# Two attentions on one core: first tokens in halves, late clearing of padding, a finer last tile

## The chip, the cores and the metric

The kernel runs on one NeuronCore of a Trainium2 chip. The core has a matrix engine (TensorE, "PE" in the profile), three engines for elementwise work (VectorE "DVE", ScalarE "ACT", GpSimd "POOL"), and a queue engine (SyncE, "SP") that issues most of the transfers. TensorE writes to PSUM[...]. The metric is the device time of one execution in microseconds, and the median of several runs is given.

## The reference

The kernel computes two attention layers, A and B, over 2048 tokens with width 640 and 32 heads of 20 columns, and puts their outputs side by side (2048 x 1280, bf16).

```python
# A: four segments of 512 tokens, causal inside a segment, with a memory M, z of the segments before
for s in range(N):
    p = softmax(qs @ ks.T * scale + causal_mask)
    a_mem = (phi(qs) @ M) / (phi(qs) @ z + 1e-06)
    o = g * a_mem + (1.0 - g) * (p @ vs)          # g = sigmoid(beta), one for each head
    M, z = M + phi(ks).T @ vs, z + sum(phi(ks))
A = concat(o) @ wo
# B: a sliding window of 256 tokens
p = softmax(where((0 <= i - j) & (i - j < 256), q @ k.T * scale, -1e9))
B = (p @ v) @ wo
```

`phi(t)` is `t + 1` where `t > 0`, else `exp(t)`.

## The kernel before

Tokens are cut into eight chunks of 512, in the order A0, B0, A1, B1, A2, B2, A3, B3. The 32 heads form eight groups of four heads (`G = 8`), and a "half" of a chunk is four groups. Nine phases each hold one or two of these halves: phase 0 is A0's first half, phase 1 is A0's second half with B0's first half, and so on to phase 8, which is B3's second half alone. `SHIFT` says how far the second half-chunk of a phase is put behind the first when their batches are interleaved.

The chain for a group of heads is this.
- **Projections.** `x` times the weights gives queries and keys with the head columns on the partitions, and values with tokens on the partitions. For most groups, queries and keys go through a store to a scratch tensor in DRAM and a spread of four loads, which puts each head on 32 partitions (`qk_job`, `bounce`). The first four groups of A0 use weights that are already padded to 32 columns a head (`wkd`, `wqd`), so they are cast directly into `kA` and `qA` (`proj_direct`).
- **Scores.** `score_batch` (L706) multiplies up to 512 columns for each of four heads into two PSUM tiles `sc`. ScalarE exponentiates each of the two (L717) into a tile `pt`. There are three `sc` tiles and six `pt` buffers (`NSC`, `NPT`). GpSimd then clears what the masks exclude (`mask`, L763 and L767).
- **Values.** `av` (L781) multiplies `pt` by the values, which carry a column of ones, so that the sum of the softmax comes out beside the result. `turn` (L804) transposes in blocks of 32 on VectorE. `norm` takes the reciprocal (L827) and multiplies (L822). `back` (L859) transposes back, and `final_job` (L895) or, for the last chunk, `last_job` (L930) does the output projection. `evac` (L235 on ScalarE, L237 on VectorE) copies PSUM to SBUF.
- **Last chunk.** Chunk B3 is handled by query tile of 128 tokens: `unit` makes three score batches of a half tile (a pair of groups with earlier keys, the diagonal blocks of all four groups, the second pair), and one "tile" entry follows them that takes the AV of the four groups into one bank, one turn of 512 columns and one norm.

All instructions are written out by a planner, which has a model of the time of each engine (`Flow`). `f.pe` is its TensorE clock. Jobs such as a projection are generators; at each step the planner takes the first job whose need is met at `f.pe`, a score batch when its keys and queries are marked done, or an AV when its masks are done. Constants named `T_W` are due times for work that waits for the first loads. `ORDER` holds one seed for each score batch. Where a seed is not zero, `pick` draws from a small random generator: it lets a job be passed over, holds a batch back, or shifts the comparison in `evac` that decides between ScalarE and VectorE. The order of each engine's queue is fixed once it is written.

The start is in `body`. SyncE loads the first chunk of `x` in three transfers (column tiles 0, 1 to 2, 3 to 4). ScalarE's queue issues the key and query weights of group 0, then `beta`. SyncE loads the padded weights of groups 1 to 3, then `wv_A`, `wk_A`, `wq_A`, the next `x` and the remaining weights. Twelve warm-up matmuls (L1157) run on a zeroed tile meanwhile. GpSimd and VectorE clear the padding of `kA`, `qA`, `qB`, `pqA`, `kB`, `MZb` and two edge tiles (L1164 to L1182), and GpSimd sets the ones in the value tiles (`v_tile`, L668 and L669). The constants made from `beta` (`consts_beta`, L304 to L320: one exponential on ScalarE and nine small VectorE instructions) and `epsv` (L289) are written out after the first planner step past `T_W[1]`.

Of the kernel before, what the change touches and what calls it, by code (L numbers as in the profile page):

```python
# [13 lines left out]
P = 128  # L14
# [14 lines left out]
    0, 768, 0, 845, 879, 493, 987, 701, 177, 0, 698, 208, 547, 919, 0, 0, 0, 989, 663, 0, 464,  # L29
    0, 0, 696, 205, 683, 935, 478, 935, 428, 909, 435, 0, 106, 0, 638, 428, 489, 780, 970, 630,  # L30
    137, 112, 487, 987, 852, 257, 438, 73, 0, 330, 618, 0, 747, 421, 0, 683, 0, 174, 542, 0,
    478, 0, 0, 0, 405, 92, 46, 310, 146, 369, 521, 643, 874, 863, 619, 683, 633, 393, 811, 875,
    892, 0, 124, 604, 814, 906, 281, 583, 0, 128, 0, 643, 307, 776, 926, 0, 727, 286, 730, 616,
    317, 955, 721, 602, 431, 787, 591, 819, 0, 635, 158, 0, 206, 0, 742, 0, 0, 232, 0, 0, 33,
    470, 435, 0, 281, 366, 583, 0, 816, 0, 0, 338, 402, 726, 607, 722, 643, 431, 417, 0, 671,
    258, 337, 208, 92, 687, 820, 129, 0, 876, 532, 783, 0, 474, 542, 646, 0, 284, 332, 0, 0,
    130, 0, 846, 102, 982, 640, 781, 0, 548, 590, 124, 838, 417, 75, 197, 0, 471, 465, 0, 331,
    690, 0, 0, 409, 0, 99, 655, 0,
)
STRETCH = 1  # L40
EW, EB = 3, 1
# [6 lines left out]
T_W = (5600.0, 7200.0, 12300.0, 12500.0, 14500.0, 16500.0)  # L48
SLACK = 500.0
SPREAD = 500.0  # L50
SHIFT = (0.0, 0.5, 0.0, 0.25, 0.0, 0.25, 0.5, 1.0, 0.0)
# [20 lines left out]
           ([(3, 6, 2, 0), (1, 2, 6, 128)], [("diag", 0, 128, 128)])]  # L72
WHOLE_B = [([(0, 0, 6, 128), (3, 6, 2, 0)], [("diag", 0, 128, 128), ("far", 384, 0, 128)]),
# [127 lines left out]
class _K:  # L201
# [149 lines left out]
    def proj_direct(self, n, w, xT, dst, g, what, ready):  # L351

        nc, f = self.nc, self.f
        yield ready
        yield "bank"
        ps, bi = self.bank()
        for kt in range(self.KT):
            nc.tensor.matmul(ps[:, :], lhsT=w[:, g, kt, :], rhs=xT[:, kt, :],
                             start=(kt == 0), stop=(kt == self.KT - 1))
            f.on_pe("full", mm_ns(512))  # L360
            if kt < self.KT - 1:
                yield 0.0
        t = self.evac(dst[:, g, :], ps[:, :], 512, 612.0)
        self.close(bi, t)
        f.open = False
        self.mark(t, n, what, g)
        self.used_x(n)
# [297 lines left out]
    def v_tile(self, name):  # L665
        v = self.big.tile([P, 2 * VH], BF16, name=name)
        for a in (0, VH):
            self.nc.gpsimd.memset(v[:, a:a + LT * VW].rearrange("p (t e) -> p t e", e=VS)[:, :, DH], 1.0)  # L668
            self.nc.gpsimd.memset(v[:, a + LT * VW:a + VH], 1.0)  # L669
        return v  # L670

    def score_batch(self, bt, kof, q):
# [43 lines left out]
        for i in range(2):  # L716
# [3 lines left out]
            self.sc_free.append(te)  # L720
        for m in masks:
            if halves:
# [30 lines left out]
    def mask(self, pt, te, kind, c0, d, w=64):  # L753

        nc, f = self.nc, self.f
        r = 8 if d else 4
# [3 lines left out]
        elif d:  # L760
            blk = pt[:].rearrange("p a (y c) -> p (a y) c", c=256)[:, :, c0:c0 + w]
# [36 lines left out]
    def turn(self, O, bi):  # L798
# [5 lines left out]
        self.nc.vector.transpose(out=tt[:], in_=O[:, :])  # L804
        self.close(bi, f.on_dve(640.0, f.pe + PE_OUT))
        return tt

    def norm(self, tt, dst, key, last):
# [3 lines left out]
        NB = L // HD  # L812
        tv = tt[:].rearrange("p (b c) -> p b c", c=HD)
        rr = self.wk.tile([P, NB], F32, name="rr", bufs=4)
        t = f.dve

        def part(out, ready=0.0):
            a, b = tv[:, :, 0:DH], rr[:].unsqueeze(2).to_broadcast([P, NB, DH])
# [5 lines left out]
            return f.on_dve(470.0, ready, True)  # L824

        def s1():
            nc.vector.reciprocal(out=rr[:], in_=tv[:, :, DH])  # L827
# [128 lines left out]
    def unit(self, n, half):  # L956
# [5 lines left out]
        if n == len(self.chunks) - 1:  # L962
            for i in range(LT):
                out = []
                if (n, half) in WHOLE:
                    for g in gs[::2]:
                        out.append([n, [(g1, (i - y, 2 * i, 2, 256 * x + 128 * (2 - y)))
                                        for x, g1 in enumerate((g, g + 1)) for y in (2, 1)],
                                    [("far", 0, 256, 128)], []])
                    out.insert(1, [n, [(g, (i, 2 * i, 2, 128 * x)) for x, g in enumerate(gs)],  # L970
                                   [("diag", 0, 256, 128), ("diag", 128, 256, 128)], []])
                    out[-1][3].append((i, gs[0]))
                    blocks.append(out)
                    continue
                for g in gs[::2]:
                    ents = []
                    for g1, c0 in ((g, 0), (g + 1, 256)):
                        ents += [(g1, (i - 2, 2 * i, 1, c0)), (g1, (i - 1, 2 * i, 2, c0 + 64)),
                                 (g1, (i, 2 * i + 1, 1, c0 + 192))]
                    out.append([n, ents, [("far", 0, 256), ("diag", 192, 256)], []])  # L980
                out.insert(1, [n, [(g, (None, i, i, 64 * x)) for x, g in enumerate(gs)],
                               [("half", 0)], []])
                out[-1][3].append((i, gs[0]))
# [482 lines left out]
```

## Time and profile before

| | |
|---|---|
| median of 8 runs | 360.54 us (360.04 to 362.11) |
| time of the profiled execution | 360.43 us |
| its span, first to last instruction | 358.4 us |
| ScalarE busy | 326.1 us (91%) |
| VectorE, GpSimd busy | 298.7 us, 222.2 us |
| first exponential of a score batch starts | 11.50 us |
| last exponential ends | 348.91 us |

A group's row in the page gives line, engine, operation, output and inputs with their shapes and the count; then busy time in us and mean ns of one; then the idle time of the engine just before and what ended it. A row of the timeline gives the start and the length in us, then the same names; a row with x5 covers five instructions that follow each other. A row of the waits gives the waiting engine and line, what ended the wait, the total in us, the number of waits and the longest.

### The profile page before, as it was taken

How to read it: one execution, taken by the hardware profiler on the slowest of the kernel's cores; microseconds unless marked ns; L12 is line 12 of the kernel's file. 1: busy time of each engine (PE TensorE's matmuls, PEld its weight loads, DVE VectorE, ACT ScalarE, POOL GpSimd, SP SyncE). 2: the span in 40 equal slices, each digit the busy share in tenths (PEclk: the TensorE clock that was granted, in tenths of full speed). 3: DMA queues.
4: the chain of work that ended last, by engine and by line, in shares of the span. 5: the costliest groups of instructions: out<-in, count | busy, mean ns of one | idle time of the engine just before them, and what ended most of it. 6: DMA issues, size and time to landing. Idle time of an engine off the chain costs nothing.

```text
span 358.4 us, 13242 instructions
## 1 busy us (share of the span) xinstructions
PE 332.5 (93%) x5515; PEld 165.9 (46%) x5515; DVE 298.7 (83%) x558; ACT 326.1 (91%) x367; POOL 222.2 (62%) x282
## 2 busy tenths in 40 slices
PE   8899999999999999989898999989999999989996
PEld 3334543544543544534433644444544544645564
DVE  6569687988998888998988987998996799899762
ACT  1797599999999999989989899999999999999991
POOL 8243146674756586492966839486269843987881
PEclk9999999999999999999999999999999999999999
DMA  7994656368374232672544203564334122112111
GB/s 243 393 380 136 194 153 167 111 194 197 103 230 115 85 98 77 211 196 84 171 148 123 64 16 98 157 163 134 102 100 142 52 80 83 52 47 90 65 50 38
DMA packets 45123, 47.90 MB, mean 134 GB/s; under 512 B 16312, under 2 KB 40696, under 8 KB 45064
## 3 DMA queue, kind: packets, MB, share of 16 engines
q1 hardware_dynamic: 44488, 46.65, 41.9%
q8 instruction: 43, 0.70, 0.9%
q10 hardware_dynamic: 576, 0.42, 0.4%
q14 instruction: 16, 0.13, 0.1%
HBM read 24.91 MB, written 19.14 MB: 123 GB/s over the span
## 4 chain that ended last, share of the span: by engine, by line
PE 48%; DVE 25%; ACT 16%; issue 6%; DMA 2%; POOL 1%; SPq 1%; ACTq 0%; DVEq 0%
ACT pt L717 15%; PE m L433 14%; PE sc L706 8%; PE m L895 8%; PE m L781 7%; PE m L619 5%; DVE tt L804 4%; DVE oD L859 3%; DVE st L237 3%; DVE o L822 2%; DVE vA L631 2%; DVE st L461 2%; DVE ot L237 2%; PE m L1057 2%; PE m L930 2%
## 5 line engine op out<-in xcount | busy, mean ns | idle before, releaser
L717 ACT ACTIVATE pt<-sc 128x1024 bf16<-128x1024 f32 (+1 forms) x344 | 307.8, 1023 | 12.1 <-PE sc L706 11.3
L767 POOL TENSOR_SCALAR_AFFINE_SELECT pt<-pt 128x512 bf16<-128x512 bf16 (+1 forms) x148 | 128.0, 868 | 124.7 <-ACT pt L717 123.7
L804 DVE STREAM_TRANSPOSE tt<-m 128x512 f32<-128x512 f32 x88 | 61.8, 709 | 20.7 <-PE m L781 19.0
L763 POOL TENSOR_SCALAR_AFFINE_SELECT pt<-pt 128x512 bf16<-128x512 bf16 (+1 forms) x80 | 72.0, 901 | 2.7 <-ACT pt L717 2.7
L237 DVE CAST st<-m 128x512 bf16<-128x512 f32 x74 | 50.2, 680 | 14.6 <-PE m L433 13.8
L706 PE MATMUL sc<-qB,kB 32*128 32x128 bf16 (+2 forms) x928 | 43.0, 248 | 3.2 <-ACT pt L717 2.5
L822 DVE TENSOR_TENSOR o<-tt,rr 128x320 bf16<-128x320 f32 x64 | 41.1, 643 | 0.5
L619 PEld LDWEIGHTS <-xT 128*128 128x128 bf16 x400 | 32.4, 97 | 17.5 <-issue 7.6
L706 PE MATMUL sc<-qA,kA 32*128 32x64 bf16 (+4 forms) x608 | 30.0, 261 | 2.1 <-DVE qA L237 1.5
L237 DVE CAST ot<-m 128x512 bf16<-128x512 f32 (+1 forms) x39 | 25.3, 650 | 6.9 <-PE m L895 4.2
L706 PEld LDWEIGHTS <-kB 32*128 32x128 bf16 x928 | 16.4, 92 | 31.4 <-issue 27.4
L895 PE MATMUL m<-wo_A,oD 128*128 128x512 bf16 (+1 forms) x160 | 26.0, 300 | 4.4 <-DVE vB L237 2.9
L895 PEld LDWEIGHTS <-oD 128*128 128x128 bf16 x280 | 19.6, 98 | 19.7 <-issue 8.2
L433 PE MATMUL m<-xT,wBq 128*128 128x512 bf16 x100 | 26.1, 380 | 2.1 <-DVE tt L804 0.7
L781 PE MATMUL m<-pt,vB 128*32 128x128 bf16 (+2 forms) x928 | 25.7, 250 | 1.9 <-DVE vA L631 0.6
L433 PE MATMUL m<-xT,wBk 128*128 128x512 bf16 x100 | 26.0, 380 | 1.6 <-DVE vA L631 0.9
L619 PE MATMUL m<-wBv,xT 128*128 128x320 bf16 (+2 forms) x200 | 26.6, 273 | 0.8 <-DVE tt L804 0.6
L619 PE MATMUL m<-wv_A,xT 128*128 128x320 bf16 (+2 forms) x200 | 26.2, 273 | 1.1 <-DVE vA L631 1.1
L781 PEld LDWEIGHTS <-vB 128*32 128x32 bf16 x928 | 17.6, 97 | 14.0 <-issue 4.5
L433 PE MATMUL m<-xT,wk_A 128*128 128x512 bf16 x90 | 23.3, 381 | 0.5 <-DVE tt L804 0.4
L859 DVE STREAM_TRANSPOSE oD<-o 128x512 bf16<-128x512 bf16 x35 | 23.4, 680 | 0.0
L781 PE MATMUL m<-pt,vA 128*32 128x448 bf16 (+5 forms) x608 | 22.2, 264 | 1.2 <-DVE st L237 1.0
(86 smaller groups left out, 363.5 us busy)
## 6 DMA issues: line engine op xcount, KB each, us to landing
out_dram<-ot SPq DMA_DIRECT2D x35, 128.0 KB
scr_kB<-st SPq DMA_DIRECT2D x20, 128.0 KB
scr_qB<-st SPq DMA_DIRECT2D x20, 128.0 KB
kB<-scr_kB SPq DMA_DIRECT2D x32, 80.0 KB
qB<-scr_qB SPq DMA_DIRECT2D x32, 80.0 KB
scr_kA<-st SPq DMA_DIRECT2D x18, 128.0 KB
scr_qA<-st SPq DMA_DIRECT2D x18, 128.0 KB
kA<-scr_kA SPq DMA_DIRECT2D x28, 80.0 KB
```

Source lines behind the costliest of these rows:

```text
L237: nc.vector.tensor_copy(out=out, in_=in_)
L433: nc.tensor.matmul(ps[:, :], lhsT=w_ap[:, kt, m * P:(m + 1) * P], rhs=xT[:, kt, :], start=(kt == 0), stop=(kt == self.KT - 1))
L619: nc.tensor.matmul(ps[:, c0:c0 + w], lhsT=xT[:, kt, tt * P:(tt + 1) * P], rhs=w_ap[:, kt, a:a + w], start=(kt == 0), stop=(kt == self.KT - 1))
L706: nc.tensor.matmul(ps[j // 2][:, j % 2, c0:c0 + 64 * nb], lhsT=k[rows, g, P * kc:P * kc + P], rhs=q[rows, g, 64 * b0:64 * (b0 + nb)], star ...
L717: nc.scalar.activation(out=pt[:, 2 * i:2 * i + 2, 0:hi], in_=ps[i][:, :, 0:hi], func=ACT.Exp, scale=self.scale)
L763: nc.gpsimd.affine_select(out=blk, in_=blk, pattern=[[0, r], [-1, w]], compare_op=ALU.is_ge, fill=self.zero, base=-1, channel_multiplier=1)
L767: nc.gpsimd.affine_select(out=blk, in_=blk, pattern=[[0, r], [1, w]], compare_op=ALU.is_ge, fill=self.zero, base=128 - w, channel_multipli ...
L781: nc.tensor.matmul(O[HD * j:HD * j + HD, c:c + 64 * nb], lhsT=self.vcols(v, h // 16 if vk[0] == "v" else 0, vt, h, HD), rhs=rhs[j], start= ...
L804: self.nc.vector.transpose(out=tt[:], in_=O[:, :])
L822: nc.vector.tensor_tensor(out=out, in0=a, in1=b, op=ALU.mult)
L859: self.nc.vector.transpose(out=self.oD[n][:, x:y, b0:b0 + nb, :].rearrange("p c b t -> p b c t"), in_=o[:, b0:b0 + nb, :].rearrange("p b ( ...
L895: nc.tensor.matmul(ps[:, P * y:P * y + w], lhsT=self.oD[n][:, m, LT * qt:LT * qt + LT, :] .rearrange("p b t -> p (b t)"), rhs=wo[:, m, a:a ...
```

## The change

The first chunk of `x` is loaded as 256 columns first (two transfers) and the other 256 columns after (one). Keys and queries of group 0 are projected in two column halves, with due times `T_W[0]` and `T_X`. A new list `FIRST` divides group 0 into three score batches, the first of which needs only the first half; group 1 gets a batch of its own for the block that it shared with group 0. Four warm-up matmuls are left out. `wv_A` is loaded after `wk_A` and `wq_A`. The jobs of A0's two halves are put into one list in the order `INIT`.

The clearing of `qB`, `pqA`, `MZb`, `kB[1]` and the edge tiles, and the ones of the `vB` tiles, go to a list `late` that is sorted by due time: each entry is written out when `f.pe` passes it. `kB[1]` and the edge tiles move from VectorE to GpSimd. `consts_beta` and `consts_eps` are in the same list.

For the last chunk, the diagonal batch comes first in each tile, also in its first half. In the last tile of the last half, the AV, turn, norm and back are done for two groups at a time, and the last mask is applied to each pair of heads after its exponential. `ORDER`, four entries of `SHIFT` and the other constants of the planner have new values.

```diff
-T_W = (5600.0, 7200.0, 12300.0, 12500.0, 14500.0, 16500.0)
+T_W = (3700.0, 6200.0, 15000.0, 10900.0, 12900.0, 16500.0)
+T_X = 5300.0
-SHIFT = (0.0, 0.5, 0.0, 0.25, 0.0, 0.25, 0.5, 1.0, 0.0)
+SHIFT = (0.0, 0.5, 0.25, 0.25, 1.0, 0.0, 0.75, 1.0, 0.0)
+INIT = ("p1", "v0", "p2", "p3", "k1", "q1", "v1")
+FIRST = [([(0, 0, 4, 0), (1, 2, 2, 256)], [("diag", 0, 256, 128)]),
+         ([(0, 4, 4, 0), (1, 4, 4, 256)], []),
+         ([(3, 6, 2, 0), (2, 4, 4, 128)], [("diag", 0, 128, 128)])]
...
-    def proj_direct(self, n, w, xT, dst, g, what, ready):
+    def proj_direct(self, n, w, xT, dst, g, what, ready, a=0, b=L):
...
-            nc.tensor.matmul(ps[:, :], lhsT=w[:, g, kt, :], rhs=xT[:, kt, :],
+            nc.tensor.matmul(ps[:, 0:b - a], lhsT=w[:, g, kt, :], rhs=xT[:, kt, a:b],
                              start=(kt == 0), stop=(kt == self.KT - 1))
...
-        t = self.evac(dst[:, g, :], ps[:, :], 512, 612.0)
+        t = self.evac(dst[:, g, a:b], ps[:, 0:b - a], b - a, 80.0 + 1.04 * (b - a))
...
+            if masks and len(masks[-1]) == 5:
+                tm = self.mask(pt, te, *masks[-1][:4], hs=(2 * i, 2 * i + 2))
...
-    def turn(self, O, bi):
+    def turn(self, O, bi, w=L):
...
+                out.append([n, [(g, (i, 2 * i, 2, 128 * x)) for x, g in enumerate(gs)],
+                            [("diag", 0, 256, 128), ("diag", 128, 256, 128)], []])
                 for g in gs[::2]:
...
+                    end = i == LT - 1 and half == 1 and g == gs[2]
+                    out.append([n, [(g1, (i - y, 2 * i, 2, 256 * x + 128 * (2 - y)))
+                                    for x, g1 in enumerate((g, g + 1)) for y in (2, 1)],
+                                [("far", 0, 256, 128) + ((1,) if end else ())], []])
+                    if end:
+                        out[-2][3].append((i, gs[0], 2))
+                        out[-1][3].append((i, gs[2], 2))
...
-        f.dve = f.pool = 4500.0
+        f.dve, f.pool = 3800.0, 6900.0
...
-        get_x(0, (1, 3))
+        xt = self.xs[0] = big.tile([P, KT, L], BF16, name="xT", bufs=2)
+        for a, b, c0 in ((0, 2, 0), (2, KT, 0), (0, KT, L // 2)):
+            nc.sync.dma_start(out=xt[:, a:b, c0:c0 + L // 2], in_=xA[0, :, a:b, c0:c0 + L // 2])
...
-        for x in range(12):
+        for x in range(8):
...
-        self.wv_A = self.load_w("wv_A", wv_A)
         self.wk_A = self.load_w("wk_A", wk_A)
         self.wq_A = self.load_w("wq_A", wq_A)
+        self.wv_A = self.load_w("wv_A", wv_A)
...
-        nc.vector.memset(self.kB[1][:].bitcast(F32), 0.0)
...
+        for x, t in enumerate((self.qB, self.pqA)):
+            clear(26500.0 + 3000.0 * x, t[:, 5:G, :].bitcast(F32), 730.0)
+        clear(28000.0, self.MZb[:], 940.0)
+        self.vB = [self.v_tile("vB%d" % x, late, 24000.0 + 12000.0 * x) for x in range(2)]
+        for g0 in range(0, G, 4):
+            clear(31000.0 + 375.0 * g0, self.kB[1][:, g0:g0 + 4, :].bitcast(F32), 950.0)
...
-                while late and f.pe > T_W[1]:
-                    late.pop(0)()
+                while late and f.pe > late[0][0]:
+                    late.pop(0)[1]()
```

## The prediction

> **What bounds the kernel now.** I read the page first, for the engine that has no slack, then ScalarE's own waits, then the stretches in which they fall.
>
> ```profile
> PE 332.5 (93%) x5515; PEld 165.9 (46%) x5515; DVE 298.7 (83%) x558; ACT 326.1 (91%) x367; POOL 222.2 (62%) x282
> ...
> L717 ACT ACTIVATE pt<-sc 128x1024 bf16<-128x1024 f32 (+1 forms) x344 | 307.8, 1023 | 12.1 <-PE sc L706 11.3
> ```
>
> ScalarE computes 344 softmax exponentials (172 score batches, two each) and is busy 326.1 of 358.4 us. A busy TensorE says less, since its ends are modelled. So I count ScalarE's 32.3 idle us. The list of its waits for the whole span:
>
> ```profile
> ACT pt L717 <- PE sc L706: 11.3, 19, 4.3
> ACT ot L235 <- PE m L930: 5.6, 3, 4.2
> ACT mz L304 <- DMA beta<-in_A_beta_dram: 3.4, 1, 3.4
> ACT vB L235 <- PE m L619: 3.2, 1, 3.2
> ACT L304 <- issue: 2.2, 1, 2.2
> ACT e L452 <- DVE pqA L461: 1.9, 1, 1.9
> ```
>
> Up to its first exponential it idles 9.9 us (2.2 + 3.4 + 4.3). Between 32.7 and 40.45 us it idles 5.7 (1.9 + 3.2 + 0.55), waiting for the second half of the first chunk. After the last exponential it idles through the tail. Only about 8 us is left, spread over 60 to 341 us. The change touches the first two and the tail. The start, from the timeline:
>
> ```profile
> 1.25 5.28 PE L1157 MATMUL m<-kB 128*128 128x512 bf16 x12 [1.25 <-DVE kB L1142]
> ...
> 6.35 1.26 PE L358 MATMUL m<-xT,pqA 128*128 128x512 bf16 x5
> ...
> 7.65 0.69 DVE L237 CAST kA<-m 128x512 bf16<-128x512 f32 x1 [1.29 <-PE m L358]
> ...
> 8.26 0.39 DVE L307 TENSOR_SCALAR mz<-mz 128x32 f32<-128x32 f32 x1
> ...
> 10.34 0.68 DVE L237 CAST qA<-m 128x512 bf16<-128x512 f32 x1
> ...
> 11.07 0.40 PE L706 MATMUL sc<-qA,kA 32*128 32x512 bf16 x4 [1.52 <-DVE qA L237]
> ...
> 11.50 4.71 ACT L717 ACTIVATE pt<-sc 128x1024 bf16<-128x1024 f32 x5 [4.35 <-PE sc L706]
> ```
>
> The first projection starts as the twelve warm-up matmuls end. Query group 0 is projected by 8.7 us, but its cast stands behind the beta constants on VectorE, 8.26 to 10.34. TensorE is idle from 9.55 to 11.07. The tail:
>
> ```profile
> 340.48 8.43 ACT L717 ACTIVATE pt<-sc 128x1024 bf16<-128x1024 f32 x9
> ...
> 349.54 1.09 POOL L763 TENSOR_SCALAR_AFFINE_SELECT pt<-pt 128x1024 bf16<-128x1024 bf16 x1
> ...
> 350.57 0.68 PEld L781 LDWEIGHTS <-vB 128*32 128x32 bf16 x48 [0.26 <-ACT ot L235]
> ...
> 351.48 0.72 DVE L804 STREAM_TRANSPOSE tt<-m 128x512 f32<-128x512 f32 x1 [2.23 <-PE m L781]
> ```
>
> The last exponential ends at 348.91; mask, value product, turn, norm, projection and store take another 9.5 us, in series.
>
> [...] warm-ups stand 0.44 us apart, the next 512-column matmuls 0.22. So fewer warm-ups means slow projections, not only early ones. [...]
>
> **The start, part by part.** Eight warm-ups instead of twelve: 1.25 + 8 x 0.44 = 4.8 us against 6.35. The first x half (327 KB) and the two first weights (328 KB) must be there: traffic starts at 1.75 us and the windows show 350 to 400 GB/s from 2.5 on, so about 4 us with the issue[...]. I take 4.8. Issues stay three for x, six and two for weights, in the same queue places. Key half, five 256-column matmuls at the slow rate: 5 x 0.21 = 1.05 plus 0.2 to finish, query half between 0.55 (fast) and 1.05: done at about 6.6. By the planner's rule with its new first seed, 18, the key half goes to VectorE, and both query halves to ScalarE: 0.586 - 256 x 0.00083 = 0.37. Scores 0.45 after that. First exponential at about 7.6 us, 3.9 earlier.
>
> This batch has 768 columns per instruction: 2 x 0.73 = 1.5 us. The beta constants come next by the planner's clock (its 6.2 us), now behind these exponentials on ScalarE and behind the second key cast on VectorE. Had the second query half been on VectorE it would wait the same 2.1 us again. On ScalarE it costs 0.23 (beta) + 0.37. So batch two starts at 7.6 + 1.5 + 0.6 + 0.45 = 10.2 us. By 11.5 ScalarE has done 2.8 us of exponentials. [...]
>
> TensorE's lead is what counts further on, because it fills 11 to 33 us almost without a break (8.50 of 8.50 us, then 9.83 of 10). Before, 14 matmuls of 512 (3.05 us) were done by 11.07. Now: 4.8 + 3.05 + 0.8 [...] = 8.65. Lead 2.4 us.
>
> **The hole at 32.7 to 40.45.** It ends when the second half's k and q are back from scratch: k projected from 24.02, the last q cast at 33.2, its spread landed near 40. TensorE's lead moves it by 2.4. Loading the k and q weights ahead of v takes 800 KB (2.0 us at 400 GB/s) off their wait, so some of their matmuls can fill in before the AV work: 0 to 1.6 more, I take 0.8. Gain 3.2 at the hole's end, bounds 1.0 and 4.6. A stall is moved, not removed: v now comes later (15.0 against 12.3 by the planner), and batch seven must wait for the first AV, as `pt` has six buffers (before: AV 21.81, scores 22.79). ScalarE will run dry near 18 us until 20.5. That is free only while the hole remains after it, which still holds over 4 us.
>
> Padding clears: 1.76 + 0.69 us leave VectorE at 3.9 to 6.4 us, where it did nothing else that mattered: 0. On GpSimd 3.9 us leave before 9 us (1.48 for the two vB tiles, 2 x 0.73 for qB and pqA, 0.94 for MZb), and 6.5 come at 24 to 37 us of the planner's clock (the same, 2 x 0.95 for kB, 0.7 for the edge tiles). It is busy 3.91 of 10 and 1.73 of 10 there, so a mask waits at most one clear (0.95), and the values behind it have no batch waiting until the hole ends: 0, at worst 1. SP has nothing behind these but the k/q spreads, whose rows were cleared before.
>
> **The tail.** The last tile's batches now run diagonal first, and the last mask is per half: 0.735 us (the 512 form) instead of a 1.15 one that started 0.6 late. Exponential to AV 0.85 instead of 1.66: 0.8. Two groups: 24 of 48 matmuls, 0.42. Turn of 256 columns: 0.26 less (slope of the 256 and 512 bf16 turns, 446 and 680). Norm 0.17, turning back 256 instead of 384 columns 0.13. Sum 1.8. VectorE's four extra instructions for the first two groups (1.1 us) fit under the last exponentials. But the third tile's ten projection matmuls, 1.52 us at 349.13, stand where the new AV wants TensorE: minus 0.3. Tail 1.5, bounds 0.8 and 2.2.
>
> **Sum.** 3.2 + 1.5 = 4.7: the profiled span 358.4 becomes 353.7, its time 360.43 becomes 355.7. The median, 360.54, is 0.1 above it: 355.8. About 0.3%, 1.1 us, is what a measurement of this kernel tells from no change.
>
> **All tie-break seeds change**, with `SHIFT` of phases 2, 4, 5 and 6. They decide which job or engine goes first at a tie. No view prices that; the 8 us of small waits and about 3 us of copies that ScalarE takes can move both ways. Zero, within 2.
>
> **Rivals.**
> - The start's gain is eaten (0.24): the half arrives late or the late v holds the queue of AVs so that q is projected no earlier. For it: the DMA share is 0.9 to 1.0 from 2.5 to 25 us, and v is 2.7 us later by plan. Against: TensorE's 1.5 idle us go in any case. Start 1.2, tail 1.2: 358.1.
> - The hole closes further and the new order saves an extra us or two (0.13): k and q projected ahead of v and of the third and fourth groups. Start 4.6, tail 2.0, order 1.5: 352.4.
> - Slower (0.13, of which 0.09 over 0.3%): the new seeds make the second projection of each phase late, so that ScalarE waits for scores at each of the six later phase ends. For it: such waits of 0.3 to 1.1 us are there already at 150 to 250 us (5.1 in ten). One 512-column projection is 1.1 us; six of them are 6.6, more than the gain. It decides above 0.8 a phase: 362.4. Against: one and a half batches stand in `sc` and six in `pt`, which cover a lateness of one projection.
> - My forecast: 0.50, its own range 354.2 to 357.3.
>
> Faster 0.50 + 0.24 + 0.13 = 0.87; within 0.3% 0.04; slower 0.09. The range for 8 in 10 leaves about 0.07 below 352.8 and 0.12 above 359.2.
>
> **What would show it.** First exponential at 7 to 8.3 us with half-rate 256-column matmuls before it; the query halves as 128x256 copies on ScalarE; a wait for scores near 18 us; the hole's end at 36 to 38.5; the last exponential 3 us or more earlier; a tail of about 8 us. Wrong if the first projection starts after 6 us, if the beta constants again stand before a query cast, if the hole still ends near 40, or if ScalarE's idle time from 60 us to the last exponential grows beyond 11 us.

## The result, and the profile after

The changed kernel takes 364.61 us (median of 11 runs, 362.66 to 365.18) against 360.5 before: a ratio of 1.0094, interval 1.0076 to 1.0112 (the two medians alone give 1.0114). The prediction, a gain to 355.8, was wrong: the kernel became slower. The profiled execution took 364.61 us, its span is 362.9 (before: 360.43 and 358.4). Beside the experiments 54 to 70% of the executions of the kernel before had a mean granted clock of 0.989 to 0.995 instead of 0.998 to 1.000, and those at 0.993 to 0.995 took 1.0 to 1.8 us longer (medians), so that its median there is 361.6 to 361.7. Ratios below are to that median; two experiments are compared with each other by their own medians and spans.

Cut at the ends of two stages, the two spans show where the time went. The "hole" is ScalarE's wait for the second half of the first chunk; it ends with the first exponential after it.

| stage | before | after | difference | predicted |
|---|---|---|---|---|
| first exponential starts | 11.50 | 8.70 | -2.80 | -3.9 |
| hole ends | 40.45 | 44.32 | **+3.87** | -3.2 |
| from there to the last exponential's end | 308.46 | 310.90 | **+2.44** | 0 |
| from there to the end of the span | 9.49 | 7.68 | **-1.81** | -1.5 |
| span | 358.4 | 362.9 | +4.5 | -4.7 |

The lines of the page that answer to those shown of before, busy time by engine and the exponentials:

```profile
PE 335.2 (92%) x5532; PEld 166.6 (46%) x5532; DVE 297.1 (82%) x555; ACT 328.7 (91%) x375; POOL 223.4 (62%) x287
...
L730 ACT ACTIVATE pt<-sc 128x1024 bf16<-128x1024 f32 (+2 forms) x346 | 308.6, 1030 | 16.8 <-PE sc L719 16.0
```

The exponentials cost what they did (308.6 us against 307.8), but the idle time before them went from 12.1 to 16.8, though the first one starts 2.8 us earlier. The waits of ScalarE from 0 to 12 us and from 40 to 60 us:

```profile
ACT pt L730 <- PE sc L719: 5.7, 2, 5.2
...
ACT vB L240 <- PE m L625: 6.1, 2, 5.5
```

The largest wait is new in its place: 5.5 us for a v projection, from 37.3 to 42.8 us, where the whole span of before had 3.2 for such a copy. The start, from the timeline of after:

```profile
1.25 3.60 PE L1183 MATMUL m<-kB 128*128 128x512 bf16 x8 [1.25 <-DVE kB L1166]
4.64 1.27 PE L363 MATMUL m<-xT,pqA 128*128 128x256 bf16 x5
...
7.99 0.39 PE L363 MATMUL m<-xT,pqA 128*128 128x256 bf16 x2 [1.39 <-DMA xT<-in_A_x_dram]
8.32 0.34 PE L719 MATMUL sc<-qA,kA 32*128 32x256 bf16 x8
8.70 1.51 ACT L730 ACTIVATE pt<-sc 128x768 bf16<-128x768 f32 x2 [5.19 <-PE sc L719]
10.36 1.06 DVE L312 TENSOR_SCALAR mz<-mz 128x32 f32<-128x32 f32 x1 [0.80 <-ACT mz L309]
13.12 0.68 DVE L242 CAST kA<-m 128x512 bf16<-128x512 f32 x1
13.85 1.24 PE L363 MATMUL m<-xT,pqA 128*128 128x512 bf16 x5 [1.03 <-DVE kA L242]
15.45 3.77 ACT L730 ACTIVATE pt<-sc 128x1024 bf16<-128x1024 f32 x4 [1.04 <-PE sc L719]
```

The first half of x was there in time: its projection starts at 4.64, right behind the eight warm-ups. The second half was not. TensorE waits 1.39 us for it, until 7.99, and the first scores stand behind the first two matmuls that need it, so they wait too though their own half is ready. Then the beta constants (VectorE, 10.36 to 13.12) stand before the key cast of group 1. Their first step takes 1.06 us, beside a mask on GpSimd that runs from 10.28 to 11.38; it took 0.39 in before. The projection of group 2's keys and, 1.04 us after the last batch, ScalarE wait behind that cast. The hole, from the timelines of after and, below it, of before:

```profile
36.67 0.74 POOL L1194 MEMSET pqA<- 128x768 f32 x1
36.82 3.43 DVE L462 TENSOR_SCALAR st<-st 128x1536 bf16<-128x1536 bf16 x1
37.34 1.84 POOL L1194 MEMSET kB<- 128x1024 f32 x2
39.13 0.38 POOL L1194 MEMSET vtopA<- 128x342 f32 x1
39.45 0.38 POOL L1194 MEMSET vbotA<- 128x342 f32 x1
40.17 0.47 DVE L637 TENSOR_TENSOR vA<-m,omg 128x320 bf16<-128x320 f32 x1
40.70 3.23 PE L625 MATMUL m<-wBv,xT 128*128 128x140 bf16 x15 [2.60 <-DVE vA L637]
44.32 4.69 ACT L730 ACTIVATE pt<-sc 128x1024 bf16<-128x1024 f32 x5
```

```profile
35.24 1.82 PE L619 MATMUL m<-wv_A,xT 128*128 128x140 bf16 x15 [0.39 <-DVE vA L631]
...
37.11 2.89 PE L619 MATMUL m<-wBv,xT 128*128 128x320 bf16 x25
...
37.77 0.55 DVE L456 TENSOR_SCALAR st<-st 128x1536 bf16<-128x1536 bf16 x1
...
39.93 0.39 PE L706 MATMUL sc<-qA,kA 32*128 32x512 bf16 x4
```

One TENSOR_SCALAR of the feature map takes 3.43 us instead of 0.55. It starts 0.15 us after a GpSimd clear and ends at 40.25, 0.4 after the last of five clears, which is about its own length. The copy of v out of PSUM (40.17) is queued behind it on VectorE, and TensorE, which waits for that copy, stands idle for 2.60 us. The matmuls after that take 3.23 us for 15 where before 15 v matmuls took 1.82. The scores that end the hole stand behind this v work in TensorE's queue, in both kernels: in before they start at 39.93, as the 25 matmuls from 37.11 end. The granted clock by stretches (the columns are busy us of PE, PEld, DVE, ACT and POOL, each with its count, then PEclk, DMA share and GB/s):

```profile
36.00:40.20 4.20, 2.10 (x29) 1.31 (x27) 4.20 (x5) 1.11 (x2) 3.83 (x6) 1.00 0.51 161
40.20:43.60 3.40, 2.90 (x14) 1.89 (x14) 2.96 (x7) 0.55 (x1) 0.00 (x0) 0.50 0.58 165
```

Half clock (0.50) for 3.4 us, just after the idle stretch; the mean over this execution is 0.995. In the tail (timeline of after) the last value product now covers 24 matmuls, and its turn 256 columns:

```profile
351.44 3.77 ACT L730 ACTIVATE pt<-sc 128x1024 bf16<-128x1024 f32 x4 [0.20 <-PE sc L719]
...
356.08 0.52 PE L799 MATMUL m<-pt,vB 128*32 128x128 bf16 x24
356.68 0.42 DVE L822 STREAM_TRANSPOSE tt<-m 128x256 f32<-128x256 f32 x1
```

The middle, from the hole's end to the end of the last exponential, in the same columns, before and then after:

```profile
40.45:348.91 308.46, 289.76 (x5143) 145.08 (x5142) 266.90 (x498) 300.35 (x337) 203.79 (x241) 1.00 0.40 119
...
44.32:355.22 310.90, 293.56 (x5177) 145.81 (x5175) 264.90 (x493) 302.02 (x343) 203.84 (x246) 1.00 0.39 115
```

Of the 2.44 us more, ScalarE is busy for 1.67 (302.02 against 300.35) and idle for 0.77. Its exponentials don't take longer; the busy part is in the copies out of PSUM that the planner gave it, seven of them instead of three.

So three things are to be explained: the hole (+3.87 where -3.2 was forecast), the middle (+2.44 where 0 was forecast), and why the early start brought nothing.

### The profile page after: what moved, and what is told of

Same layout as the page of the kernel before. It is cut to its first block, busy times and chain, and to the rows that moved or that the text cites. A ratio compares the mean times of both kernels' runs of the same rounds, so it can differ in the third digit from the quotient of the medians.

```text
span 362.9 us, 13282 instructions
## 1 busy us (share of the span) xinstructions
PE 335.2 (92%) x5532; PEld 166.6 (46%) x5532; DVE 297.1 (82%) x555; ACT 328.7 (91%) x375; POOL 223.4 (62%) x287
## 2 busy tenths in 40 slices
DMA packets 46019, 47.90 MB, mean 132 GB/s; under 512 B 16312, under 2 KB 41848, under 8 KB 45960
## 4 chain that ended last, share of the span: by engine, by line
PE 38%; ACT 31%; DVE 19%; issue 5%; DMA 3%; POOL 2%; SPq 1%; DVEq 0%; ACTq 0%; POOLq 0%
ACT pt L730 30%; PE m L439 13%; PE sc L719 7%; PE m L799 6%; PE m L625 5%; DVE tt L822 4%; PE m L913 3%; DVE st L242 2%; DVE o L840 2%; DMA xT<-in_A_x_dram 2%; DVE st L462 1%; PE m L363 1%; PE m L948 1%; DVE u L840 1%; DVE vA L637 1%
## 5 line engine op out<-in xcount | busy, mean ns | idle before, releaser
L730 ACT ACTIVATE pt<-sc 128x1024 bf16<-128x1024 f32 (+2 forms) x346 | 308.6, 1030 | 16.8 <-PE sc L719 16.0
L785 POOL TENSOR_SCALAR_AFFINE_SELECT pt<-pt 128x512 bf16<-128x512 bf16 (+1 forms) x148 | 127.6, 864 | 127.3 <-ACT pt L730 126.4
L822 DVE STREAM_TRANSPOSE tt<-m 128x512 f32<-128x512 f32 (+1 forms) x89 | 62.1, 702 | 19.0 <-PE m L799 17.4
L781 POOL TENSOR_SCALAR_AFFINE_SELECT pt<-pt 128x512 bf16<-128x512 bf16 (+1 forms) x81 | 69.7, 863 | 4.2 <-ACT pt L730 4.1
L719 PE MATMUL sc<-qB,kB 32*128 32x128 bf16 (+2 forms) x928 | 42.0, 248 | 2.0 <-ACT pt L730 1.5
L840 DVE TENSOR_TENSOR o<-tt,rr 128x320 bf16<-128x320 f32 (+1 forms) x65 | 41.3, 635 | 0.8
L625 PE MATMUL m<-wBv,xT 128*128 128x320 bf16 (+2 forms) x200 | 28.3, 283 | 5.0 <-DVE vA L637 2.6
L719 PE MATMUL sc<-qA,kA 32*128 32x320 bf16 (+5 forms) x616 | 30.4, 260 | 1.7 <-ACT pt L730 1.3
L242 DVE CAST ot<-m 128x512 bf16<-128x512 f32 (+1 forms) x37 | 23.8, 648 | 8.8 <-PE m L913 6.2
L439 PE MATMUL m<-xT,wq_A 128*128 128x512 bf16 x90 | 24.0, 381 | 0.7 <-ACT st L240 0.4
L799 PE MATMUL m<-pt,vA 128*32 128x320 bf16 (+5 forms) x616 | 22.2, 262 | 1.4 <-DVE st L242 1.3
L799 PEld LDWEIGHTS <-vB 128*32 128x32 bf16 x928 | 17.7, 97 | 12.1 <-issue 4.8
```

The source lines that it names most:

```text
L242: nc.vector.tensor_copy(out=out, in_=in_)
L439: nc.tensor.matmul(ps[:, :], lhsT=w_ap[:, kt, m * P:(m + 1) * P], rhs=xT[:, kt, :], start=(kt == 0), stop=(kt == self.KT - 1))
L625: nc.tensor.matmul(ps[:, c0:c0 + w], lhsT=xT[:, kt, tt * P:(tt + 1) * P], rhs=w_ap[:, kt, a:a + w], start=(kt == 0), stop=(kt == self.KT - 1))
L719: nc.tensor.matmul(ps[j // 2][:, j % 2, c0:c0 + 64 * nb], lhsT=k[rows, g, P * kc:P * kc + P], rhs=q[rows, g, 64 * b0:64 * (b0 + nb)], star ...
L730: nc.scalar.activation(out=pt[:, 2 * i:2 * i + 2, 0:hi], in_=ps[i][:, :, 0:hi], func=ACT.Exp, scale=self.scale)
L781: nc.gpsimd.affine_select(out=blk, in_=blk, pattern=[[0, r], [-1, w]], compare_op=ALU.is_ge, fill=self.zero, base=-1, channel_multiplier=1)
```

## The experiments

My theory after the two traces: the late clears lengthen the VectorE instruction in the hole (3.43 us instead of 0.55), and the rest of the loss is the start (x, beta) and the order of the middle. The rivals: the halves of x are themselves the loss; the beta constants are; the copies on ScalarE are.

**The clears at the start again.** The memsets, and the ones of the `vB` tiles, are issued where the kernel before has them; the planner's clock still counts them late, so the order of all other work stays that of after.

```diff
...
         def clear(t, ap, ns):
-            def go():
-                nc.gpsimd.memset(ap, 0.0)
-                f.on_pool(ns)
-            late.append((t, go))
+            (nc.vector if t > 30000.0 else nc.gpsimd).memset(ap, 0.0)
+            late.append((t, lambda: f.on_pool(ns)))
```

> The padding is cleared at the start again, on the engines and in the places of the kernel before; every other queue keeps its order. Theory 1 (the late clears on GpSimd hold up VectorE: the TENSOR_SCALAR of the st tile took 3.43 us instead of 0.55 while clears ran, and the v cast behind it held TensorE's bank): that instruction takes 0.6 us again, the first exponential after the hole comes at about 41.4 us instead of 44.3, and the time falls by 2.9 us to 361.7. Theory 2 (the late second half of x and the beta constants set the hole's end): the time falls by less than 0.5 us. Theory 3 (the new seeds put copies on ScalarE): no change.

Measured: 360.96 us (20 runs), ratio 0.9977, interval 0.9961 to 0.9993; span 359.2. The timeline of this kernel in the hole:

```profile
37.14 0.50 DVE L462 TENSOR_SCALAR st<-st 128x1536 bf16<-128x1536 bf16 x1
...
38.35 1.84 PE L625 MATMUL m<-wBv,xT 128*128 128x140 bf16 x15
...
40.57 3.77 ACT L728 ACTIVATE pt<-sc 128x1024 bf16<-128x1024 f32 x4
```

The same instruction takes 0.50 us, the 15 matmuls 1.84, the hole ends at 40.57: 3.75 earlier than in after, and the span is 3.7 shorter. Only the place of these memsets differs between the two (and for `kB[1]` and the edge tiles the engine), so they are the cause; 1.4 of the 3.75 is the half clock (3.23 us for the 15 matmuls at 0.50, against 1.84 at 1.00). What is left is a kernel about level with before. How a clear holds the instruction up is not shown: the trace of after has only its 3.43 us, from 0.15 us after the start of the first of five clears in a row to 0.4 after the end of the last.

Against before, by the same stages: hole +0.1, middle +2.5, tail -1.8. The early start is still worth nothing at the hole's end, and the middle still costs 2.5.

**Late clears in the kernel before.** Only the clears of `qB`, `pqA`, `MZb`, `kB[1]` and the edge tiles, with the due times of the change.

```diff
-        for t in (self.qB, self.pqA):
-            nc.gpsimd.memset(t[:, 5:G, :].bitcast(F32), 0.0)
...
+        for x, t in enumerate((self.qB, self.pqA)):
+            clear(26500.0 + 3000.0 * x, t[:, 5:G, :].bitcast(F32))
```

> The kernel before with qB, pqA, MZb, kB and the edge tiles cleared late on GpSimd, at the due times of the change; no other queue changes its order. Theory 1: the clears meet the TENSOR_SCALAR of phi on VectorE at 33.8 or 37.8 us, which takes up to 3 us longer, and TensorE waits behind it: 2 to 4 us slower than before. If late clears are harmless by themselves: within 0.5 us.

Measured: 360.65 us (12 runs), ratio 0.9981, interval 0.9967 to 0.9995; span 359.3. Timeline of this kernel:

```profile
33.32 0.95 POOL L1168 MEMSET MZb<- 128x1024 bf16 x1
33.82 1.27 DVE L456 TENSOR_SCALAR pqA<-kA 128x512 bf16<-128x512 bf16 x1
34.21 0.74 POOL L1168 MEMSET pqA<- 128x768 f32 x1
...
38.80 0.55 DVE L456 TENSOR_SCALAR st<-st 128x1536 bf16<-128x1536 bf16 x1
```

The loss of 2 to 4 us that theory 1 gave did not come. The same lengthening is there, in a cheaper place: beside two of the clears another TENSOR_SCALAR takes 1.27 us instead of 0.27; TensorE then waits 1.39 us for VectorE instead of 0.39, without a half clock after it (the 15 matmuls take 1.82 us, as in before; the mean granted clock is 0.999), and the hole ends at 41.47, 1.0 later than in before. The median doesn't show that 1.0 as a loss. The large one (38.80) comes when the clears are over and takes 0.55. So a late clear is not costly as such. What it costs is set by the VectorE instruction that it happens to meet and by what is queued behind that.

**x in whole rows again.** The first chunk loads in three transfers by column tile; everything else as in after.

```diff
-        for a, b, c0 in ((0, 2, 0), (2, KT, 0), (0, KT, L // 2)):
-            nc.sync.dma_start(out=xt[:, a:b, c0:c0 + L // 2], in_=xA[0, :, a:b, c0:c0 + L // 2])
+        for a, b in ((0, 1), (1, 3), (3, KT)):
+            nc.sync.dma_start(out=xt[:, a:b, :], in_=xA[0, :, a:b, :])
```

> The first chunk of x comes in whole rows again (three transfers by column tile); the order of all engines stays. Theory 2: the first projection starts near 5.8 us instead of 4.6, but the wait for the second half until 7.95 is gone, the first exponential comes no later than 8.7, and the time falls by 1.0 to 1.4 us. Theory 1: what is won at the start is lost again behind the clears, change within 0.5 us. Theory 3: no change.

Measured: 365.64 us (4 runs), ratio 1.0131, interval 1.0069 to 1.0194. First exponential 9.67 (after: 8.70), hole's end 44.22 (44.32). Against the 364.61 of after, four runs from 363.65 to 369.09 show no clear difference. The gain of theory 2 did not come: with whole rows the first scores come 1.0 later, and the hole stays, with the same TENSOR_SCALAR at 3.44 us ahead of its end. So the halves are not the loss, at least while the clears set the hole's end.

**The halves contiguous in memory.** On the kernel with early clears, with the first chunk laid out half by half, so that a half is read in pieces of 1024 to 2560 bytes instead of 512.

```diff
-            nc.sync.dma_start(out=xt[:, a:b, c0:c0 + L // 2], in_=xA[0, :, a:b, c0:c0 + L // 2])
+            nc.sync.dma_start(out=x4[:, y, a:b, :], in_=xA0[:, y, a:b, :])
```

> Early clears as in e1_clears_early, and the two halves of the first x laid out contiguous in memory and in the tile, so that the same three transfers have pieces of 1024, 1536 and 2560 bytes instead of 512. If the pieces make the second half late, it lands near 6 us instead of 7.6 to 8, the first exponential comes at 7.0 to 7.6 us instead of 9.0, and the time falls by up to 1.4 us against e1_clears_early; if the beta constants then take the gain, less than 0.4 us in the time with the first exponential early all the same. If the second half is late for another reason, the first exponential stays at 8.4 us or later.

Measured: 360.22 us (20 runs) against 360.96 with early clears alone; ratio 0.9973, interval 0.9956 to 0.9989. Timeline of this kernel:

```profile
6.70 0.38 PE L379 MATMUL m<-xT,pqA 128*128 128x256 bf16 x2
...
7.59 1.51 ACT L744 ACTIVATE pt<-sc 128x768 bf16<-128x768 f32 x2 [4.09 <-PE sc L733]
...
12.74 1.24 PE L379 MATMUL m<-xT,pqA 128*128 128x512 bf16 x5 [1.03 <-DVE kA L258]
```

TensorE doesn't wait for the second half here, and the first exponential is at 7.59, where I had predicted it; it was 9.03 with early clears alone. The hole ends at 39.14, 1.43 earlier. These two profiles are the extremes: the first exponential starts at 7.93 to 9.03 in the seven profiles with 512-byte pieces and at 7.59 to 7.93 in the three with contiguous halves, so 1.43 is the upper end of what the layout gives. The beta constants still cost TensorE its 1.03 us before group 2. The last exponential ends 0.6 earlier only.

**The beta constants later.** On after, due at 13.0 us of the planner's clock.

```diff
-        late = [(T_W[1], self.consts_beta), (T_W[1], self.consts_eps)]
+        late = [(13000.0, self.consts_beta), (13000.0, self.consts_eps)]
```

> The constants from beta are written out later (due at 13.0 instead of 6.2 us of the planner's clock), so they stand behind four casts of groups 1 and 2 on VectorE. Theory 2: TensorE's idle 1.0 us before 13.85 and ScalarE's 1.0 us before 15.45 go, the time falls by about 1 us. Theory 1: the hole's end does not move by more than 0.5 us, since the clears run there anyway. Theory 3: no change.

Measured: 367.78 us (5 runs), ratio 1.0179, interval 1.0148 to 1.021. Timeline:

```profile
18.03 1.06 DVE L312 TENSOR_SCALAR mz<-mz 128x32 f32<-128x32 f32 x1 [2.08 <-ACT mz L309]
...
21.71 0.59 PE L439 MATMUL m<-xT,wk_A 128*128 128x512 bf16 x1 [3.69 <-DVE kA L242]
...
29.09 0.63 ACT L458 ACTIVATE e<-kA 128x512 bf16<-128x512 bf16 x1 [8.57 <-DVE pqA L467]
```

Group 1's casts are freed, but beta stands on ScalarE behind ten exponentials instead of two, VectorE waits 2.08 us for it, and the casts of group 3 stand behind that: TensorE idles 3.69 us and has half its clock from 20.1 to 26.9 (its weight loads start 0.43 us apart from 22.09 on, and the mean granted clock is 0.991), ScalarE idles 8.57, and the hole, in which the TENSOR_SCALAR beside the clears takes 3.44 us again, ends at 47.71. The wait moved to a worse place.

**The beta constants earlier.** On the kernel with early clears, due at 4.85 us.

```diff
-        late = [(T_W[1], self.consts_beta), (T_W[1], self.consts_eps)]
+        late = [(4850.0, self.consts_beta), (4850.0, self.consts_eps)]
```

> Early clears as in e1_clears_early, and the constants from beta written out right after the first query cast, so that they fall into the time in which VectorE and ScalarE wait for the second half of x. If the start is what keeps the hole's end at 40.6 us, TensorE's idle 1.0 us before 13.85 and ScalarE's 1.0 before 15.45 go and the time falls by 1.0 us against e1_clears_early. If the hole's end depends on something else (the order of v, AV and the k/q projections), less than 0.4 us.

Measured: 361.57 us (20 runs), ratio 1.0009, interval 0.9986 to 1.0033. Timeline:

```profile
7.05 1.60 DVE L312 TENSOR_SCALAR mz<-mz 128x32 f32<-128x32 f32 x1
...
10.34 0.42 DVE L242 CAST kA<-m 128x256 bf16<-128x256 f32 x1
10.81 1.02 PE L363 MATMUL m<-xT,pqA 128*128 128x512 bf16 x4 [1.51 <-DVE kA L242]
```

Now they stand before the second key half, and their first step takes 1.60 us (0.39 in before) beside memsets on GpSimd (the clear of `MZb` and the ones of `vB`, up to 8.61). The hole ends at 40.19, 0.4 earlier; no gain in time.

**No beta constants at all.** On the kernel with early clears, two GpSimd memsets set the gate's constants, so this kernel leaves out the gate's dependence on `beta`.

```diff
-        nc.scalar.activation(out=e, in_=self.beta[:], func=ACT.Exp, scale=-1.0)
...
+        nc.gpsimd.memset(self.omg[:], 0.5)
+        nc.gpsimd.memset(self.g8[:], 1.0)
```

> Early clears as in e1_clears_early, and the constants from beta left out: the gate is a constant set on GpSimd, so ScalarE's one and VectorE's eight small instructions at 10.4 to 12.8 us are gone. If they are what eats TensorE's lead at the start, TensorE's idle 1.0 us before 13.85 goes, the hole's end comes 1.0 us earlier and the time falls by about 1 us against e1_clears_early. If TensorE's lead is lost to the order of v and AV, less than 0.4 us.

Measured: 360.33 us (20 runs), ratio 0.998, interval 0.9959 to 1.0001. First exponential 8.03, hole's end 38.39, 2.2 earlier than with beta; but x landed about 1.0 earlier as well in this profile, so the two are mixed, although both kernels load x in the same pieces. To part them:

**Contiguous halves and no beta constants**, the last two edits together.

```diff
+        self.xs[0] = Halves(x4)
...
+        nc.gpsimd.memset(self.omg[:], 0.5)
+        nc.gpsimd.memset(self.g8[:], 1.0)
```

> The run with early clears and contiguous halves, and with the beta constants left out too (the gate is a constant, so that part of the computation is missing). In the run without beta alone, x also landed 1.0 us earlier, so its gain of 2.2 at the end of the hole mixes two things; here there is no wait for x in either kernel. Theory (beta's chain on VectorE holds TensorE back by about 1.2 us, whatever x does): the casts of group 1 follow their matmuls, no idle TensorE before group 2's keys, the end of the hole at 37.9 (37.6 to 38.2) against 39.14, which would be within 0.7 of the 37.25 that I predicted for the change; last exponential 0.5 to 1.2 earlier than 350.96. Rival (beta only fills time in which TensorE's queue would wait anyway, and the 2.2 was the earlier landing): the end of the hole at 38.7 to 39.2, the last exponential within 0.4 of 350.96.

Measured: 359.91 us (20 runs), ratio 0.9951, interval 0.9934 to 0.9968. From the timeline of this kernel:

```profile
7.93 1.51 ACT L731 ACTIVATE pt<-sc 128x768 bf16<-128x768 f32 x2 [4.43 <-PE sc L720]
...
37.84 0.39 PE L720 MATMUL sc<-qA,kA 32*128 32x512 bf16 x4
...
38.30 9.27 ACT L731 ACTIVATE pt<-sc 128x1024 bf16<-128x1024 f32 x10
```

The hole ends at 38.30, 0.84 earlier than with contiguous halves alone: between what the theory and the rival expected. The first scores came 0.34 later in this profile (7.93 against 7.59); counted from the first exponential the hole ends 30.37 us on, against 31.55, which is 1.2 less. So beta's chain costs 0.8 us there as measured, and 1.2, as the theory had it, only if the late first batch is set aside. The time fell by 0.3 only. The last exponential ends 0.6 later than with beta (351.57 against 350.96), but the profiled run, 360.95, is the slowest of the 20.

What becomes of the gains is read from ScalarE's groups between 45 and 345 us, shapes kept apart: early clears; contiguous halves; no beta; both.

```profile
L728 ACT ACTIVATE pt<-sc 128x1024 bf16<-128x1024 f32 x282 | 264.4, 1075 | 8.9 <-PE sc L717 8.1
...
L744 ACT ACTIVATE pt<-sc 128x1024 bf16<-128x1024 f32 x281 | 264.0, 1073 | 9.3 <-PE sc L733 8.4
...
L715 ACT ACTIVATE pt<-sc 128x1024 bf16<-128x1024 f32 x280 | 262.6, 1073 | 10.2 <-PE sc L704 9.6
...
L731 ACT ACTIVATE pt<-sc 128x1024 bf16<-128x1024 f32 x279 | 262.1, 1069 | 10.6 <-PE sc L720 9.8
```

The earlier the hole ends (40.57, 39.14, 38.39, 38.30), the longer ScalarE then waits for scores: 8.9, 9.3, 10.2, 10.6 us (the last in that slowest of 20 runs). Of 2.27 us at the hole's end, 1.05 is left in the median (360.96 to 359.91).

**The copies of the middle on VectorE.** After has 6 copies of 500 or 512 columns on ScalarE between 45 and 345 us (3.80 us), before 3 (1.92), so they were suspected of the 2.4 us. On after, all copies of 512 columns go to VectorE: five of these six and one after 345 us.

```diff
-            nc.scalar.copy(out=out, in_=in_)
+            (nc.vector.tensor_copy if n == 512 else nc.scalar.copy)(out=out, in_=in_)
```

> The six 512-column copies out of PSUM that ScalarE takes go to VectorE, in the same places; the order of the rest stays. Theory 3 (ScalarE sets the pace from 45 us to the last exponential, and the seeds gave it three such copies more than before): the six are 3.9 us of ScalarE's time, the time falls by 2 to 3.9 us. Rival to it (VectorE is just as tight there, 0.68 us for each): less than 1 us. Theories 1 and 2 alone: no change.

Measured: 367.42 us (4 runs), ratio 1.016, interval 1.0116 to 1.0205. The gain of 2 to 3.9 us did not come: the time is 2.8 above after. ScalarE is rid of the copies and waits longer for scores, between 100 and 200 us 6.6 us instead of 2.4; a part of that falls beside a second stretch of half clock, 3.4 us from 121.5, which the profile of after doesn't have (mean granted clock 0.991 against 0.995). So giving the copies to VectorE is no remedy. That they cost nothing where they stand is not shown: in after they are the larger part of the 2.44. Why the scores come later here is not shown either; the projections behind the moved copies may come later.

**The order of before in the middle.** On the kernel with early clears: the first 11 seeds of after, then those of before, and before's `SHIFT`.

```diff
-    18, 563, 0, 0, 221, 35, 0, 347, 263, 0, 166, 385, 0, 49, 899, 317, 201, 716, 0, 886, 0,
+    18, 563, 0, 0, 221, 35, 0, 347, 263, 0, 166, 698, 208, 547, 919, 0, 0, 0, 989, 663, 0, 464,
...
-SHIFT = (0.0, 0.5, 0.25, 0.25, 1.0, 0.0, 0.75, 1.0, 0.0)
+SHIFT = (0.0, 0.5, 0.0, 0.25, 0.0, 0.25, 0.5, 1.0, 0.0)
```

> Early clears as in e1_clears_early; the seeds from the twelfth batch on and the shifts are those of the kernel before. The part from the hole's end to the last exponential is 2.5 us longer in e1_clears_early than in the kernel before. If the new seeds and shifts cost that, the time falls by 2 to 2.5 us against e1_clears_early. If seeds only fit the schedule they were chosen for, it stays or gets longer.

Measured: 359.23 us (6 runs), ratio 0.9944, interval 0.9918 to 0.997; 1.7 less than with after's order. The same group row of ScalarE, 45 to 345 us:

```profile
L717 ACT ACTIVATE pt<-sc 128x1024 bf16<-128x1024 f32 x287 | 268.8, 1082 | 4.2 <-PE sc L706 3.5
```

Idle time before these exponentials is 4.2 us instead of 8.9 (7.2 in before). The last one ends at 347.05 instead of 351.56, but the tail is 10.65 us instead of 7.64, because 48 value matmuls and 33 of the output projections are left for the end, instead of 24 and 15: 4.5 gained, 3.0 given back. So the new seeds with `SHIFT` cost 1.7 us against the old ones, in waits: from the hole's end to the last exponential ScalarE is busy for 301.75 us here and for 301.88 with after's order. This is not the middle of before again, which has fewer copies and longer waits. Seeds and `SHIFT` were not parted.

**The new tail alone, on before.**

```diff
-                    ps_ = [p for x in range(4) for p in parts[(n, g[1] + x)]
+                    ps_ = [p for x in range(g[2]) for p in parts[(n, g[1] + x)]
```

(with the last chunk's batches, `mask`, `turn` and `norm` of the change)

> The kernel before with the new last chunk alone (diagonal batch first, last tile by two groups, last mask by pairs of heads). The tail after the last exponential was 9.5 us before and 7.7 after: 1.8 us faster than before. If the new order of batches costs ScalarE waits ahead of the last exponential, less than 1 us faster.

Measured: 359.2 us (4 runs), ratio 0.9953, interval 0.9937 to 0.997; span 357.4. Last exponential's end 348.7, tail 8.7. The span is 1.0 shorter than before, 0.7 in the tail and 0.2 ahead of it, so alone the new tail wins little more than half of the 1.8 expected.

**Everything that helped**: early clears, contiguous halves, the order of before after 11 seeds, the new tail; beta as in after.

```diff
+        self.xs[0] = Halves(x4)
...
+    18, 563, 0, 0, 221, 35, 0, 347, 263, 0, 166, 698, 208, 547, 919, 0, 0, 0, 989, 663, 0, 464,
```

> e6_before_order with the contiguous halves of e10_x_contig. If both gains are real they add up: below 0.9944 of the kernel before, by what e10_x_contig wins over e1_clears_early. If the start's gain is lost before the hole's end, the same as e6_before_order within 0.2%.

Measured: 358.73 us (11 runs), ratio 0.992, interval 0.9897 to 0.9943; span 356.7; the first exponential starts at 7.81, the hole ends at 39.37. That is 0.5 us less than without the contiguous halves (359.23), so the two gains add up, and it beats both kernels.

## Why the prediction was wrong

Between the span forecast, 353.7, and the one measured, 362.9, lie 9.2 us. The clears are 3.75 of them, the gain at the hole's end that did not come 3.3, the middle 2.4; the tail was 0.3 better than forecast. So two steps failed, the price of the clears and the gain at the hole, and the seeds, taken at zero, cost something too.

- **Padding clears, "0, at worst 1": the step that failed first.** It looked at who uses GpSimd and found a mask that waits at most one clear. What took longer was an instruction of VectorE: 0.55 became 3.43 us, then 2.60 us of idle TensorE, then 15 matmuls at half clock. Undone, it is 3.75 us at the hole's end and 3.65 in the median. The prediction did not ask what VectorE runs in that stretch; in before no clear runs beside this TENSOR_SCALAR (37.77, 0.55 us). It had also set the stretch aside because no batch waits there "until the hole ends"; but the late copy of v stood in front of the very scores that end it.
- **The hole, "gain 3.2": the second step that failed.** With the clears aside it was -0.1 (40.57 against 40.45). Contiguous halves give 1.43 and no beta 0.84 more; with all three the hole ends at 38.30, 2.15 earlier than in before, and 1.05 is still missing to the 37.25 forecast. No run parts TensorE's lead from the weights' order, but the traces say much. From its first projection to the scores that end the hole TensorE is busy for 31.20 of 33.58 us in before (6.35 to 39.93) and for 32.60 of 33.20 with all three (4.64 to 37.84): 1.71 earlier, 1.78 less idle, 1.40 more work, as the new order has 299 matmuls there instead of 273. That leaves a lead of 2.09 of the 2.4 forecast, and the hole's end follows it. The weights' order, priced at 0.8, shows no gain: in both kernels those scores start as TensorE ends the v projection ahead of them. By the trace's semaphore times the spread of q lands some 0.05 us before them in both, so two limits meet there, and to have k and q projected ahead of v eases only one. That is read from the traces and not tested. The "start's gain is eaten" rival was right about the late half.
- **"First exponential at about 7.6".** It came at 8.70. The first half and the projection were right (4.64 against 4.8). The term left out was the second half of x: it was taken to be under way while the first half is worked on, was there for TensorE at 7.99, and stood in front of the first scores in TensorE's order. With contiguous halves it is 7.59 to 7.93.
- **The beta constants.** Priced against group 0 only ("had the second query half been on VectorE"). They held group 1's casts instead: 1.03 us of TensorE, 0.8 to 1.2 at the hole's end.
- **A gain at the hole's end counted in full.** Under half of 2.27 us came through to the median. ScalarE waits for scores later instead. Why the later phases don't follow the earlier start was not settled; that it depends on the order is shown by the runs with before's seeds, whose waits between 45 and 345 us are 4.2 us with contiguous halves and without.
- **"Tie-break seeds: zero, within 2".** The middle of after is 2.44 longer, mostly by copies on ScalarE, which the prediction had named as able to "move both ways". Against before's seeds, under the new start, they cost with `SHIFT` 1.7 us in the median, the longer tail of the other order taken off. The slower rival put this at 6.6 us of late second projections. From 60 us to the last exponential ScalarE's idle time is 8.4 us against 7.9, so that rival had the sign but neither the place nor the price of the main loss.
- **The tail, "1.5, bounds 0.8 and 2.2".** 1.8 measured in after, 1.8 with early clears, and on before alone 0.7 of it in the tail and 0.2 ahead of it. The steps hold: the last value product starts 0.87 after the last exponential (0.85 forecast), with 24 matmuls, and 256 columns are turned. The size holds only with this order: with before's seeds the same code has a tail of 10.65.

## What to carry to other kernels

Before work is moved to an idle engine, list what the other engines run in that stretch; GpSimd's idle time beside VectorE was not free here (0.55 us became 3.43). A loss is set by what is met there: clears at the same due times cost nothing measurable in one kernel and 3.7 us in another. Gains at the start have to be followed to the last exponential, and a batch that needs half of a transfer had better not be queued behind work that needs the other half (read off the trace; no run here puts that batch first).

## What the runs showed of the hardware

- A VectorE TENSOR_SCALAR took longer beside GpSimd memsets: 3.43 us instead of 0.55 beside five clears in a row, 1.27 instead of 0.27 beside two, and the small 32-column one 1.60 instead of 0.39. Beside a mask on GpSimd the small one took 1.06 in three profiles (after, beta later, contiguous halves). Not every overlap shows it: the 0.39 in before starts at 8.26, beside memsets that end at 8.60.
- 2.60 us of idle TensorE were followed by 3.4 us at half clock (granted clock 0.50), which added 1.4 us to that stall. Such a stall is not always followed by it: with x in whole rows the same TENSOR_SCALAR takes 3.44 us in the hole, and the granted clock from 40 to 60 us is 1.00; with early clears alone TensorE is idle for 2.24 us before 8.32, and the mean granted clock of that execution is 1.000.
- The eight warm-ups of 512 columns in after start about 0.43 us apart. The first five projections of 256 columns right behind them take 1.27 us, five of the same from 8.93 on 0.71.
- TensorE had the second half of x at 7.2 to 8.3 us in the seven profiles with pieces of 512 bytes, and at 7.2 or before in the three with pieces of 1024 to 2560 bytes and 896 pieces fewer in the queue (45123 packets in all against 46019). So pieces of 512 tended to be slower in this place, by less than the first pair of profiles suggests; whether it was the pieces' size or their count was not tried.
